# The first token transform on the quarters of the array, with rows loaded by parity

## The chip, the cores and the metric

The kernel runs on one core of one Trainium2 chip. The metric is the device time of one execution in microseconds (us); lower is better. A core has a matrix engine (PE, with its own queue of weight loads, PEld), a vector engine (DVE), a scalar engine (ACT), GpSimd (POOL), a queue that only issues transfers (SP), and 16 DMA engines that all transfers share. SBUF is the memory on the core, 128 partitions wide; PSUM, eight banks of 512 floats in each of 128 partitions, takes the results of PE.

## What is computed

The input x has 2048 tokens of 512 channels (S, D). The reference, cut to what matters:

```python
def _A_ref(x, w_r, w_i):                       # a filter in the spectrum
    X = jnp.fft.rfft2(x, axes=(-2, -1)) * (w_r + 1j * w_i)
    return jnp.fft.irfft2(X, s=(S, D), axes=(-2, -1))

def _B_ref(x, w1, b1, w2, b2):                 # an MLP over the tokens
    h = _layernorm(x)
    u = _gelu(jnp.einsum("bsd,sf->bdf", h, w1) + b1)       # F = 1792
    return (jnp.einsum("bdf,fs->bds", u, w2) + b2).transpose(0, 2, 1)

xn = _layernorm(x)
out = x + _A_ref(xn, w_r, w_i) * _silu(_B_ref(xn, w1, b1, w2, b2))
```

All arrays are 32-bit floats: x and the output 4 MB each, w1 and w2 14.7 MB each, the filter 2.1 MB for each of its two parts.

## The kernel before

**Layout.** Token 16q + j stands at partition q of row block j, so there are 16 row blocks x[:, j] of 128 tokens by 512 channels, and w1[:, j] holds the matching rows of w1. The 1792 columns of w1 are 14 blocks of 128 (NF). The transform over the tokens is split in two steps: a 128-point transform over q within each row block (the first token transform), and 16-point transforms over j later.

**GEMM1** sums, for each of the 14 blocks of w1, over the 16 row blocks. Every operand is split into a high and a low part in a shorter format (ACT makes the high part, DVE the low one), and each product is three matmuls of 128x512: high by high, high by low, low by high. One block takes one PSUM bank, so the blocks go in three groups: the first with the row blocks as they arrive, two more afterwards.

**First stage (lines 429 to 516), a loop over the row blocks j.** For each j: SP loads x[:, j] (load_x, up to five ahead) and two pieces of w1[:, j] (w1_load: WA, four blocks from block 0; WB, three from block 7; three buffers each); DVE and ACT make the mean, the spread and the normalised rows (stats, spreads, scales, normed) and the high and low parts; PE runs 21 matmuls of GEMM1 into banks 0 to 6 (hidden_early) and between them the first token transform into bank 7: four matmuls of 128x128 by 128 columns in full 32-bit floats, where the rows are the weights and a table of cosines and sines, cf (scaled by turned), streams past. ACT copies bank 7 to zt (first_copy), and DVE and POOL add and subtract its quarters into ey (fold). In six of the sixteen passes a further piece of w1 for the second group (w1e, four blocks in two loads of two) is loaded and split ahead of its use. SP also copies x into the output in four pieces, to which results are added at the end.

**Middle (lines 518 to 736).** The last two groups of GEMM1, four blocks (4, 5, 10, 11) and then three (6, 12, 13), run over the same 16 row blocks, in steps of one block and one row block (hidden_rest, hidden). Their w1 pieces, w1s, are loaded up to eight steps ahead (w1_ahead) into four and then five buffers. In between PE runs the filter for eight pairs of frequencies (filter_pair): channel transforms of 128x128, a 16-point transform on 64-row halves (gf), the product with the filter on DVE, and the way back, which is 32 matmuls of 64x64 weights by 64 columns spread over the four quarters of the array (hf by xc). PACE says how many steps of GEMM1 stand between the pieces of the filter. The activation (gelu) and the parts for GEMM2 (forms) follow each block that is complete. The last four row blocks of the last group are kept to the end (LATE, last_sum).

**GEMM2 (line 739 to the end)** runs in 128x256 matmuls with sums of quarters of w2, whose pieces SP and POOL load as buffers come free, with the inverse channel and token transforms (channels, spectral) between.

**What sets the order.** A scheduler orders each engine's instructions; those in keep(...) stand as written. Each engine takes its own in order, SP too: a load that waits for a free buffer holds back all that SP has behind it.

The functions that the diff touches, and what calls them:

Of the kernel before, what the change touches and what calls it, by code (L numbers as in the profile page):

```python
# [3 lines left out]

# [4 lines left out]
F32 = mybir.dt.float32  # L9
# [12 lines left out]
FORMS = (2, 1, 0, 3, 4, 5, 6)  # L22
# [4 lines left out]
PACE = [(2, 2, 2, 1, 1, 1)] * 4 + [(2, 2, 2, 2, 1, 1)] * 4  # L27
# [5 lines left out]
LATE = 12  # L33
# [23 lines left out]
def _constants():  # L57
    q = np.arange(P)
    f = np.zeros((P, P))
    for lo in range(16):  # L60
        for hi in range(4):
            k = _k1(lo, hi)
            a = 2 * np.pi * ((q * k) % P) / P
            f[:, lo * 8 + 2 * hi] = np.cos(a)
            f[:, lo * 8 + 2 * hi + 1] = np.cos(np.pi * q) if k == 0 else np.sin(a)
# [14 lines left out]
    for lo in range(16):  # L80
        for hi in range(4):
            k1, (n, l), (t, h) = _k1(lo, hi), divmod(lo, 2), divmod(hi, 2)
            for r in range(16):
# [14 lines left out]
                rows = slice(64 * t, 64 * t + 64)  # L98
                p = [l * 64 + 2 * (h * 16 + r) + c for c in range(2)]
# [10 lines left out]
    for lo in range(16):  # L110
        for t in range(2):
            rows = slice(64 * (lo % 2), 64 * (lo % 2) + 64)
            v = back[lo // 2, t, rows].reshape(64, 2, 2, 16, 2)
            back[lo // 2, t, rows] = np.einsum("psajb,abhc->pshjc", v, _pairs(lo, t).reshape(2, 2, 2, 2)).reshape(64, 2, 64)

    b = f.T.reshape(32, 2, 2, P)
    even, odd = b[:, 0, :, 0::2].copy(), b[:, 0, :, 1::2].copy()
    even[0], odd[0] = (b[0, 0, 0, 0::2], b[0, 1, 0, 0::2]), (b[0, 0, 0, 1::2], b[0, 1, 1, 1::2])  # L120
    ft = np.concatenate([np.concatenate([v.reshape(64, 64) for v in (even, odd)], 1)] * 2)
# [23 lines left out]
def spectral_mixer_kernel(tc, x, w1, b1, w2, b2, wk, we, wx, c_f, c_ft, c_d, c_i, c_g, c_h, c_t, out):  # L145
# [19 lines left out]
    with tc.tile_pool(name="ps", bufs=1, space=PSUM) as psp, ExitStack() as left, ExitStack() as right:  # L165
        ps = psp.tile([P, 8, 512], F32, name="ps")
        pers = pool(left, "left", "pers", 1)
        cf = pers.tile([P, P], F32, name="cf")
# [75 lines left out]
        def new_h(j):  # L244
            return lnp.tile([P, D], F32, name=f"h{j}", tag="h")

        def turned(j, m, i):

            c = lnp.tile([P, P], F32, name=f"cf{j}", tag="cfj")
            keep(A.activation(c, cf, AF.Copy, scale=m["q"][:, i]))  # L250
            return c

        def first_transform(h, c):
            z = ps[:, 7].rearrange("p (b c) -> p b c", c=P)

            for b, k in enumerate((0, 1, 3, 2)):
                T.matmul(z[:, b], h[:, k * P:(k + 1) * P], c, start=True, stop=True)  # L257
# [16 lines left out]
        def w1_load(j, f0, nf, up, wide):  # L274
            raw = (w1r if up is w1p else up).tile([P, wide * P], F32, name=f"w1r{f0}_{j}", tag="w1r", bufs=3)
            SY.dma_start(raw[:, :nf * P], w1[:, j, f0 * P:(f0 + nf) * P])
# [103 lines left out]
        BATCHES = ((((4, 2), (10, 2)), 4, (7, 2, 0, 1)), (((6, 1), (12, 2)), 3, (7, 0, 1)))  # L380
        w1_early, pairs = {}, {}

        def w1_runs(i, where):
            f = 0
            for f0, nf in BATCHES[i // NJ][0]:
                last = SY.dma_start(where[:, f:f + nf * P], w1[:, i % NJ, f0 * P:(f0 + nf) * P])
# [64 lines left out]
        folds = iter(())  # L451
        for j in range(NJ):
# [18 lines left out]
            z = hidden_early(j, 4, 0, w[0], lambda: first_transform(h, c))  # L471
            hidden_early(j, 3, 4, w[1], lambda: None)
# [43 lines left out]
            folds = fold(j, first_copy(j, z))  # L516
# [531 lines left out]
```

## Time and profile before

| | |
|---|---|
| median of 3 runs | 375.73 us |
| lowest and highest | 375.49 and 379.15 us |
| the profiled execution, as timed | 375.0 us |
| its span in the trace | 373.2 us |
| granted TensorE clock, mean | 0.994 |
| first stage | 7.19 to 98.41 us |
| middle | 98.41 to 207.40 us |
| GEMM2 | 207.40 to 373.2 us |

The profiled execution took 375.0 us, 1.8 us more than the span from its first to its last instruction. It lies 0.7 us under the median. The first stage begins with the first matmul of GEMM1, after 16 matmuls on zeros; the middle with the first matmul on w1e; GEMM2 with the first on parts of w2.

How to read the lines: "x24 | 58.5, 398" is 24 instructions, 58.5 us busy together, 398 ns for one. A line number is that of the kernel; L142 is a helper that records many operations, so there the names of the tiles tell them apart. In the table of stretches each engine has its busy time and its count, and the last three columns are the granted clock, the mean busy share of the 16 DMA engines and the GB/s that they moved. A full-precision matmul shows as two records in the trace.

### The profile page before, as it was taken

Reading aid. Unit: us, or ns where it says so; the run is one execution under the profiler, and the core shown is the slowest. Engines: PE = TensorE matmul, PEld = TensorE weight load, DVE = VectorE, ACT = ScalarE, POOL = GpSimd, SP = SyncE. Lnnn points to the kernel's source line nnn. Section 1 sums busy time; section 2 is a strip of 40 time slices with the busy share of each in tenths; the row PEclk is TensorE's granted clock in tenths of the full one; section 3 lists DMA queues with packets and bytes.
Section 4 is the critical chain, followed back from the end, with each engine's and each line's share of the span. In section 5 each row is a group of like instructions: output and inputs, shape, how many; then the busy total and the mean of one; then the engine's idle time right before and its main releaser. Section 6 shows DMA issues by size and latency. Waiting matters only on the chain.

```text
span 373.2 us, 7614 instructions
## 1 busy us (share of the span) xinstructions
PE 364.3 (98%) x2888; PEld 316.0 (85%) x2888; DVE 296.7 (79%) x565; ACT 212.0 (57%) x381; POOL 84.5 (23%) x123
## 2 busy tenths in 40 slices
PE   8999999999999999999999999999999999999991
PEld 4888888888877777778788999899998989898981
DVE  6799887864298999999999978596868687777871
ACT  4686668654773444456537776545565646564530
POOL 1133322132222221122111001040405050413131
PEclk9999999999999999999999999999999999999997
DMA  7884779304266565787638587897879788887443
GB/s 237 279 293 155 244 240 314 117 0 126 77 191 191 178 226 184 246 259 222 201 84 264 146 232 155 240 134 236 153 212 178 202 188 191 195 190 154 76 56 56
DMA packets 34404, 68.35 MB, mean 183 GB/s; under 512 B 4656, under 2 KB 17856, under 8 KB 34240
## 3 DMA queue, kind: packets, MB, share of 16 engines
q1 hardware_dynamic: 25920, 43.09, 36.1%
q0 software_dynamic: 8448, 24.78, 31.1%
q8 instruction: 22, 0.36, 0.4%
q14 instruction: 14, 0.11, 0.1%
HBM read 59.47 MB, written 8.13 MB: 181 GB/s over the span
## 4 chain that ended last, share of the span: by engine, by line
PE 98%; DVE 0%; POOL 0%; ACT 0%; issue 0%; POOLq 0%
PE ps L142 72%; PE ps L420 21%; PE ps L257 4%; PE ps L409 2%; DVE rows L142 0%; POOL wz L397 0%; ACT g L142 0%; POOLq L1037 0%
## 5 line engine op out<-in xcount | busy, mean ns | idle before, releaser
L142 DVE TENSOR_TENSOR w2f<-a,w2f 128x896 fp32r<-128x896 f32 x36 | 39.3, 1092 | 24.6 <-ACT w2f L142 24.5
L420 PE MATMUL ps<-h,w1h 128*128 128x512 f32 x224 | 58.5, 398 | 0.0
L142 PE MATMUL ps<-h,w1h 128*128 128x512 f32 x176 | 56.2, 401 | 0.0
L420 PEld LDWEIGHTS ps<-h,w1h 128*128 128x128 f32 x224 | 40.9, 188 | 7.9
L142 ACT ACTIVATE w2f<-a 128x896 fp32r<-128x896 f32 x36 | 36.8, 1021 | 12.2 <-issue 6.7
L142 PE MATMUL ps<-fb,w2f 128*128 128x256 f32 x336 | 41.5, 278 | 0.0
L142 PE MATMUL ps<-fa,w2f 128*128 128x256 f32 x336 | 41.0, 277 | 0.0
L142 PEld LDWEIGHTS ps<-h,w1h 128*128 128x128 f32 x176 | 31.6, 188 | 10.7 <-issue 4.9
L142 PEld LDWEIGHTS ps<-fb,w2f 128*128 128x128 f32 x336 | 39.4, 188 | 0.9 <-issue 0.8
L142 PE MATMUL ps<-fc,w2f 128*128 128x256 f32 x336 | 39.6, 276 | 0.0
L142 PEld LDWEIGHTS ps<-fa,w2f 128*128 128x128 f32 x336 | 39.5, 188 | 0.0
L142 POOL DMA_DIRECT2D s<-in_w_dram x14 | 18.2, 1299 | 93.1 <-DMA s<-in_w_dram 60.0
L142 PEld LDWEIGHTS ps<-fc,w2f 128*128 128x128 f32 x336 | 38.9, 188 | 0.0
L142 PE MATMUL ps<-h,w1l 128*128 128x512 f32 x88 | 34.4, 391 | 0.0
L420 PE MATMUL ps<-h,w1l 128*128 128x512 f32 x112 | 30.6, 389 | 0.0
L142 POOL DMA_DIRECT2D out_dram<-r x28 | 23.7, 1285 | 29.8 <-DVE r L142 29.8
L270 POOL TENSOR_TENSOR ey<-t 128x256 f32<-128x256 f32 x16 | 15.7, 982 | 55.1 <-DVE t L268 55.1
L415 DVE TENSOR_TENSOR w1l<-w1r,w1h 128x512 fp32r<-128x512 f32 (+1 forms) x32 | 20.8, 651 | 7.0 <-ACT w1h L412 6.7
L420 PEld LDWEIGHTS ps<-h,w1l 128*128 128x128 f32 x112 | 21.0, 188 | 4.6
L262 ACT ACTIVATE zt<-ps 128x512 f32<-128x512 f32 x16 | 9.5, 595 | 26.2 <-PE ps L257 26.2
L602 POOL DMA_DIRECT2D xc<-xc x16 | 9.8, 620 | 64.0 <-ACT xc L600 47.1
L142 DVE TENSOR_TENSOR w2f<-s,w2f 128x896 fp32r<-128x896 f32 x15 | 16.3, 1088 | 7.9 <-ACT w2f L142 7.9
(115 smaller groups left out, 684.5 us busy)
## 6 DMA issues: line engine op xcount, KB each, us to landing
a<-in_w_dram SPq DMA_DIRECT2D x22, 448.0 KB, 3.8
wt<-in_wk_dram POOLq DMA_DIRECT2D x16, 512.0 KB, 5.1
s<-in_w_dram SPq DMA_DIRECT2D x16, 448.0 KB, 4.0
s<-in_w_dram POOLq DMA_DIRECT2D x16, 448.0 KB, 6.3
w1s<-in_w_dram SPq DMA_DIRECT2D x36, 128.0 KB, 2.8
w1r<-in_w_dram SPq DMA_DIRECT2D x16, 256.0 KB, 4.1
xc<-xc POOLq DMA_DIRECT2D x16, 256.0 KB, 3.0
x<-in_x_dram SPq DMA_DIRECT2D x15, 256.0 KB, 3.3
```

The costliest lines, as they stand in the source:

```text
L142: return lambda *args, **kw: self.keep(operation(*args, **kw))
L257: T.matmul(z[:, b], h[:, k * P:(k + 1) * P], c, start=True, stop=True)
L262: keep(A.activation(zt, z, AF.Copy))
L270: G.tensor_add(ey[:, 0::3, :, j], a, b)
L409: T.matmul(ps[:, 0], wz[:, :P], wz, start=True, stop=True)
L415: keep(V.tensor_sub(dst, src, hi.bitcast(F32)))
L420: T.matmul(ps[:, bank + i], w[wi][:, i * P:(i + 1) * P], hj, start=first and j == 0, stop=last and j == NJ - 1)
L602: keep(G.dma_start(*(v.rearrange("p s t c -> p s (t c)") for v in (there[c::2], here[1 - c::2, ::-1]))))
```

## The change

- **Rows by parity.** Every load of x (first stage) and of w1 goes through by_parity: its source pattern is read as [2, 64, columns], even rows first, so that partitions 0 to 63 hold the even rows of a block and 64 to 127 the odd ones. It is still one load. GEMM1 sums over all rows, so the order does not matter there, as long as x and w1 have the same.
- **First token transform on quarters.** The table cf shrinks from 128x128 to 128x64. A 64-point transform is made of the even rows and of the odd rows apart: sixteen matmuls of 64x64 weights by 64 columns for a row block, two row halves (e, to banks 6 and 7) by two halves of the channels (m) by four blocks of channels. Two row blocks are done behind one another, at every odd j; the last two, 14 and 15, singly. The two halves are put together in the later 16-point tables (gf), where the pairs of frequencies are now formed. ACT's copy of a row block (first_copy) reads both banks and writes runs of two; one copy follows at the end of each pass, so the folds come a pass later for half of the row blocks.
- **GEMM1's blocks six, four, four.** Bank 6 is needed by the transform, so the first stage carries six blocks (0 to 2 and 7 to 9) in place of seven: 18 matmuls a pass. The last two groups have four blocks each (3, 4, 10, 11 and 5, 6, 12, 13), each loaded in two loads of two blocks; the second group had three, of one and two. w1s has four buffers throughout. PACE, LATE, FORMS and the places of gelu are set to the new groups.

The diff, cut to its core:

```diff
-FORMS = (2, 1, 0, 3, 4, 5, 6)
+FORMS = (2, 0, 1, 3, 4, 5, 6)
-PACE = [(2, 2, 2, 1, 1, 1)] * 4 + [(2, 2, 2, 2, 1, 1)] * 4
+PACE = [(2, 2, 2, 2, 2, 1)] * 8
-LATE = 12
+LATE = 4
...
-    f = np.zeros((P, P))
-    for lo in range(16):
-        for hi in range(4):
-            k = _k1(lo, hi)
-            a = 2 * np.pi * ((q * k) % P) / P
-            f[:, lo * 8 + 2 * hi] = np.cos(a)
-            f[:, lo * 8 + 2 * hi + 1] = np.cos(np.pi * q) if k == 0 else np.sin(a)
+    a = 2 * np.pi * (np.outer(q, np.arange(32)) % P) / P
+    f = np.stack([np.cos(a), np.sin(a)], 2)
+    f[0::2, 0, 1], f[1::2, 0, 1] = np.cos(np.pi * q[0::2] / 2), np.sin(np.pi * q[1::2] / 2)
+    f = np.concatenate([f[0::2], f[1::2]]).reshape(P, 64)
...
+                out[:, rows] = np.einsum("sajb,abhc->shjc", out[:, rows].reshape(2, 2, 16, 2),
+                                         _pairs(lo, t).reshape(2, 2, 2, 2)).reshape(2, 64)
...
-        cf = pers.tile([P, P], F32, name="cf")
+        cf = pers.tile([P, 64], F32, name="cf")
...
+        def by_parity(to, src):
+            return SY.dma_start(to, src.rearrange("(q e) c -> e q c", e=2))
         def load_x(j):
             xs[j] = lnp.tile([P, D], F32, name=f"x{j}", tag="x", bufs=5)
-            SY.dma_start(xs[j], x[:, j])
+            by_parity(xs[j], x[:, j])
...
-            return lnp.tile([P, D], F32, name=f"h{j}", tag="h")
+            return lnp.tile([P, D], F32, name=f"h{j}", tag="h", bufs=3)
         def turned(j, m, i):
-            c = lnp.tile([P, P], F32, name=f"cf{j}", tag="cfj")
+            c = lnp.tile([P, 64], F32, name=f"cf{j}", tag="cfj", bufs=3)
             keep(A.activation(c, cf, AF.Copy, scale=m["q"][:, i]))
             return c
-        def first_transform(h, c):
-            z = ps[:, 7].rearrange("p (b c) -> p b c", c=P)
-            for b, k in enumerate((0, 1, 3, 2)):
-                T.matmul(z[:, b], h[:, k * P:(k + 1) * P], c, start=True, stop=True)
-            return z
+        def first_transform():
+            for r, (j, h, c) in reversed(list(enumerate(normal, 2 - len(normal)))):
+                z = ps[:, 6:8, 256 * r:256 * r + 256].rearrange("p e (b c) -> p e b c", b=4)
+                for b, k in enumerate((0, 1, 3, 2)):
+                    for m in range(2):
+                        for e in range(2):
+                            rows, at = slice(64 * e, 64 * e + 64), k * P + 64 * m
+                            T.matmul(z[64 * m:64 * m + 64, e, b], h[rows, at:at + 64], c[rows], start=True, stop=True)
+                transformed.insert(0, (j, z))
+            normal.clear()
         def first_copy(j, z):
             zt = lnp.tile([P, 4, P], F32, name=f"zt{j}", tag="zt")
-            keep(A.activation(zt, z, AF.Copy))
+            keep(A.activation(zt.rearrange("p b (s e c) -> p e (b s) c", e=2, c=2), z.rearrange("p e b (s c) -> p e (b s) c", c=2),
+                              AF.Copy))
             return zt
         def fold(j, zt):
@@ -272,8 +276,8 @@
             yield
         def w1_load(j, f0, nf, up, wide):
-            raw = (w1r if up is w1p else up).tile([P, wide * P], F32, name=f"w1r{f0}_{j}", tag="w1r", bufs=3)
-            SY.dma_start(raw[:, :nf * P], w1[:, j, f0 * P:(f0 + nf) * P])
+            raw = (w1r if up is w1p else up).tile([P, nf * P], F32, name=f"w1r{f0}_{j}", tag="w1r", bufs=3)
+            by_parity(raw[:, :nf * P], w1[:, j, f0 * P:(f0 + nf) * P])
...
-        BATCHES = ((((4, 2), (10, 2)), 4, (7, 2, 0, 1)), (((6, 1), (12, 2)), 3, (7, 0, 1)))
+        BATCHES = (3, (7, 2, 0, 1)), (5, (2, 7, 0, 1))
         w1_early, pairs = {}, {}
-        def w1_runs(i, where):
-            f = 0
-            for f0, nf in BATCHES[i // NJ][0]:
-                last = SY.dma_start(where[:, f:f + nf * P], w1[:, i % NJ, f0 * P:(f0 + nf) * P])
-                f += nf * P
+        def w1_blocks(i, where):
+            f0 = BATCHES[i // NJ][0]
+            for a in range(2):
+                f = (f0 + NH * a) * P
+                last = by_parity(where[:, 2 * P * a:2 * P * (a + 1)], w1[:, i % NJ, f:f + 2 * P])
             return last
         def w1_early_load(i):
             if i % 2 == 0:
                 pairs[i // 2] = usp.tile([P, 2, D], F32, name=f"w1e{i}", tag="u")
-            w1_runs(i, pairs[i // 2][:, i % 2])
+            w1_blocks(i, pairs[i // 2][:, i % 2])
...
-        WA, WB = (0, 4, w1p, 4), (NH, 3, wbp, 3)
+        WA, WB = (0, 3, w1p, 4), (NH, 3, wbp, 3)
         xs[0] = lnp.tile([P, D], F32, name="x0", tag="x", bufs=5)
         halves = slice(0, D // 2), slice(D // 2, D)
         for c_ in halves:
-            SY.dma_start(xs[0][:, c_], x[:, 0, c_])
+            by_parity(xs[0][:, c_], x[:, 0, c_])
...
-        folds = iter(())
+        folds, normal, transformed, copied_rows = iter(()), [], [], []
+        def next_fold():
+            j, z = transformed.pop(0)
+            return fold(j, first_copy(j, z))
...
-            z = hidden_early(j, 4, 0, w[0], lambda: first_transform(h, c))
-            hidden_early(j, 3, 4, w[1], lambda: None)
+            normal.append((j, h, c))
+            hidden_early(j, 3, 0, w[0], first_transform if j % 2 or j == NJ - 2 else lambda: None)
+            hidden_early(j, 3, 3, w[1], lambda: None)
...
-            folds = fold(j, first_copy(j, z))
+            if transformed:
+                copied_rows.append(next_fold())
+                if j == NJ - 3:
+                    copied_rows.append(next_fold())
+                folds = chain(*(copied_rows.pop(0) for _ in range(1 + (j == NJ - 2))))
...
-            n = BATCHES[i // NJ][1] * P
-            if i == NJ:
-                w1_stage.close()
-                w1_raw[0] = pool(lstage, "left", "w1b", 5)
-            loaded[i] = w1_raw[0].tile([P, n], F32, name=f"w1s{i}", tag="w1s")
-            last = w1_runs(i, loaded[i])
+            loaded[i] = w1_raw[0].tile([P, 4 * P], F32, name=f"w1s{i}", tag="w1s")
+            last = w1_blocks(i, loaded[i])
...
-                while ahead and ahead[0] < max(i + AHEAD + (ahead[0] >= NJ), NE + 4):
+                while ahead and ahead[0] < max(i + AHEAD, NE + 4):
                     w1_ahead(ahead.pop(0))
-                j, banks = i % NJ, BATCHES[i // NJ][2]
-                if i == 2 * NJ - LATE // 3:
+                j, banks = i % NJ, BATCHES[i // NJ][1]
+                if i == 2 * NJ - LATE:
...
-        def last_sum(ft, k, bank):
-            for n in range(LATE // 3):
-                hidden(NJ - LATE // 3 + n, k, bank, w1_parts[n])
+        def last_sum(k, bank):
+            for n in range(LATE):
+                hidden(NJ - LATE + n, k, bank, w1_parts[n])
...
-        last_sum(12, 1, 0)
+        last_sum(0, 2)
+        gelu(5, 2)
+        last_sum(2, 0)
...
-        last_sum(13, 2, 1)
+        last_sum(3, 1)
-        last_sum(6, 0, 7)
+        last_sum(1, 7)
```

The first place is SP's queue in the first stage, where the loads of row blocks 2 to 4 stand: x is a row block, w1r a piece of w1 (WA, then WB), in_x_dram and in_w_dram are the arrays in memory, and the last column is the pattern of the destination, partitions first. Before:

```order
L276 DMA w1r_2_281<-in_w_dram 128x512
L276 DMA w1r_2_283<-in_w_dram 128x384
L200 DMA x_331<-in_x_dram 128x512
L276 DMA w1r_3_335<-in_w_dram 128x512
L276 DMA w1r_3_337<-in_w_dram 128x384
L276 DMA w1r_4_410<-in_w_dram 128x512
L465 DMA cd<-in_c_d_dram 128x512
```

The same place now:

```order
L193 DMA w1r_2_272<-in_w_dram 128x1x384
L193 DMA w1r_2_274<-in_w_dram 128x1x384
L193 DMA x_342<-in_x_dram 128x1x512
L193 DMA w1r_3_346<-in_w_dram 128x1x384
L193 DMA w1r_3_348<-in_w_dram 128x1x384
L193 DMA w1r_4_414<-in_w_dram 128x1x384
L474 DMA cd<-in_c_d_dram 128x512
```

The loads stand in the same order and number; the pattern of each load by parity now has three counts, the table cd still two, and the first piece of w1 is a quarter smaller.

The second place is PE in the first stage, row blocks 3 and 4: w1h and w1l are the high and low parts of w1, h those of the rows (or, beside cf, the rows as weights). Before:

```order
L420 MATMUL ps<-h_93,w1h_4_439 128x512 x4
L420 MATMUL ps<-h_93,w1l_4_440 128x512 x4
L257 MATMUL ps<-cf_457,h_443 128x128 x4
L420 MATMUL ps<-h_93,w1h_4_439 128x512 x4
L420 MATMUL ps<-h_93,w1h_4_441 128x512 x3
L420 MATMUL ps<-h_93,w1l_4_442 128x512 x3
L420 MATMUL ps<-h_93,w1h_4_441 128x512 x3
```

Now:

```order
L424 MATMUL ps<-h_92,w1h_3_368 128x512 x3
L424 MATMUL ps<-h_92,w1l_3_369 128x512 x3
L259 MATMUL ps<-cf_398,h_372 64x64 x16
L259 MATMUL ps<-cf_339,h_330 64x64 x16
L424 MATMUL ps<-h_92,w1h_3_368 128x512 x3
L424 MATMUL ps<-h_92,w1h_3_370 128x512 x3
L424 MATMUL ps<-h_92,w1l_3_371 128x512 x3
L424 MATMUL ps<-h_92,w1h_3_370 128x512 x3
L424 MATMUL ps<-h_93,w1h_4_468 128x512 x3
```

A pass has 18 matmuls of GEMM1 in place of 21; every second pass has two transforms of sixteen small matmuls, the others none.

More of the change, by code (lines that the diff above doesn't have):

```diff
@@ L3 @@
 from contextlib import ExitStack
+from itertools import chain
 import concourse.bass as bass
@@ L107, in _constants @@
     freq = freq.reshape(P, 16)
[L110 to L121, printed above, removed]
+    ft = np.concatenate([np.concatenate([f[:64].T, f[64:].T], 1)] * 2)
     c = {
@@ L660, in spectral_mixer_kernel @@
         todo = []
-        late = []
         def form_step():
-            while late:
-                gelu(*late.pop())
             while todo and held[0] + 2 <= passed[0]:
@@ L670, in form_step @@
                 todo.pop(0)
-                late.extend(waiting.pop(0) if waiting else ())
         def hidden_rest():
@@ L695, in hidden_rest @@
                     todo.extend([forms(3), forms(4)])
-                    waiting.append([(5, 2)])
-        def last_sum(ft, k, bank):
-            for n in range(LATE // 3):
-                hidden(NJ - LATE // 3 + n, k, bank, w1_parts[n])
+        def last_sum(k, bank):
+            for n in range(LATE):
+                hidden(NJ - LATE + n, k, bank, w1_parts[n])
         order = [1, 2, 0, 3, 4, 5, 6, 7]
         wts = [weights(2 * order[0])]
-        chain = [filter_pair(n) for n in order]
+        filters = [filter_pair(n) for n in order]
         rest = hidden_rest()
@@ L715, in advance @@
                 else:
-                    next(chain[what[0]])
-        next(chain[0])
-        gelu(9, 6)
+                    next(filters[what[0]])
+        next(filters[0])
+        gelu(9, 5)
         todo.extend(forms(i) for i in FORMS[:3])
-        waiting = [[(3, 3)]]
         advance([START])
-        gelu(8, 5)
-        gelu(7, 4)
+        gelu(7, 3)
+        gelu(8, 4)
         for n in range(8):
```

12 lines of the change are left out of this document (5 added, 7 removed).

## The prediction

> **What bounds the kernel now.** I read the page first: the busy shares, the DMA row of the forty slices, the queues, the chain of work that ended last.
>
> ```profile
> span 373.2 us, 7614 instructions
> PE 364.3 (98%) x2888; PEld 316.0 (85%) x2888; DVE 296.7 (79%) x565; ACT 212.0 (57%) x381; POOL 84.5 (23%) x123
> DMA  7884779304266565787638587897879788887443
> q1 hardware_dynamic: 25920, 43.09, 36.1%
> PE 98%; DVE 0%; POOL 0%; ACT 0%; issue 0%; POOLq 0%
> ```
>
> PE is the bound: it is busy for 98% of the span, and 98% of the chain runs through it. The transfers are hidden, but not by a wide margin: many slices have the DMA engines at 70 to 90%. The queue that SP feeds (q1) moved 43.09 MB and kept sixteen engines busy for 36.1% of 373.2 us, which is 2156 engine-us, so one engine moves 20.0 GB/s. Next the stretches, for the three stages (busy time and count of PE, PEld, DVE, ACT, POOL, then the granted clock, the DMA share and GB/s):
>
> ```profile
> 7.19:98.41 91.22, 91.22 (x467) 77.55 (x465) 69.00 (x187) 59.37 (x125) 23.51 (x34) 1.00 0.58 189
> 98.41:207.40 108.99, 108.99 (x1042) 85.90 (x1041) 101.64 (x179) 61.20 (x113) 22.21 (x39) 1.00 0.65 202
> 207.40:373.20 165.80, 158.18 (x1369) 150.42 (x1367) 122.29 (x187) 88.23 (x140) 37.66 (x44) 0.99 0.74 167
> ```
>
> In the first stage and the middle PE never stops. What the change saves there on PE counts in full, as long as nothing else becomes longer.
>
> **The change on PE.** Two passes of the first stage, and the one place where 32 small matmuls on the quarters stand between full matmuls (start, length, what):
>
> ```profile
> 66.10 1.05 PE L257 MATMUL ps<-cf,h 128*128 128x128 f32 x8
> ...
> 68.62 0.84 PE L420 MATMUL ps<-h,w1l 128*128 128x512 f32 x3
> ...
> 71.79 1.05 PE L257 MATMUL ps<-cf,h 128*128 128x128 f32 x8
> ...
> 185.49 0.39 PE L142 MATMUL ps<-h,w1l 128*128 128x512 f32 x1
> 185.81 1.16 PE L142 MATMUL ps<-hf,xc 64*64 64x64 f32 x64
> 186.90 0.73 PE L142 MATMUL ps<-h,w1h 128*128 128x512 f32 x2
> 187.47 0.40 PE L142 MATMUL ps<-h,w1l 128*128 128x512 f32 x1
> ```
>
> From 68.62 to 71.79 fourteen matmuls of GEMM1 start, 0.2264 us each. A pass lasts 71.79 - 66.10 = 5.69 us; 21 matmuls are 4.75 of it, so a transform costs 0.93. On the quarters, from 185.49 to 187.47, there are three matmuls of GEMM1 (0.68) and 32 small ones of exactly the shape that two row blocks will need: 1.98 - 0.68 = 1.30 us, with the changes of shape in it. Seven pairs save 7 x (2 x 0.93 - 1.30) = 3.9 us. A single transform of sixteen lies between half of 1.30 and all of it, 0.65 to 1.30 against 0.93; I take the middle, no gain, and keep 0.6 us a side for the two together. The number of GEMM1's matmuls is unchanged (14 blocks by 16 by 3); 48 of them, 10.9 us, move from the first stage to the middle. So PE's work falls by 3.9 us, 3.3 to 4.5. ACT's copy and DVE's folds keep their number and size; they move by up to a pass, off PE's path.
>
> **The change on the loads.** This is where I expect the time to be decided. The sizes before (count, KB each, median us to landing):
>
> ```profile
> wt<-in_wk_dram POOLq DMA_DIRECT2D x16, 512.0 KB, 5.1
> w1s<-in_w_dram SPq DMA_DIRECT2D x36, 128.0 KB, 2.8
> w1r<-in_w_dram SPq DMA_DIRECT2D x16, 256.0 KB, 4.1
> xc<-xc POOLq DMA_DIRECT2D x16, 256.0 KB, 3.0
> x<-in_x_dram SPq DMA_DIRECT2D x15, 256.0 KB, 3.3
> out_dram<-in_x_dram SPq DMA_DIRECT2D x4, 960.0 KB, 7.1
> w1r<-in_w_dram SPq DMA_DIRECT2D x16, 192.0 KB, 4.6
> w1e<-in_w_dram SPq DMA_DIRECT2D x12, 128.0 KB, 3.8
> hf<-in_c_h_dram SPq DMA_DIRECT2D x8, 128.0 KB, 2.2
> w1s<-in_w_dram SPq DMA_DIRECT2D x16, 64.0 KB, 3.2
> gf<-in_c_g_dram SPq DMA_DIRECT2D x8, 64.0 KB, 2.0
> x<-in_x_dram SPq DMA_DIRECT2D x2, 128.0 KB
> ```
>
> The x, w1r, w1e and w1s rows add up to 18.87 MB, all of x and w1, and all of it now goes by parity. Before, each such load counts 128 rows first, on both sides. By parity the source counts 2 first, each with 64 rows a step of two apart; the destination still counts 128 partitions. What a load is cut along decides on how many DMA engines it runs. Loads that count 128 first do fill sixteen, as three stretches show (same columns as above):
>
> ```profile
> 20.00:24.00 4.00, 4.00 (x23) 3.46 (x22) 3.72 (x15) 3.39 (x9) 1.62 (x2) 1.00 0.96 295
> 88.00:94.00 6.00, 6.00 (x32) 5.11 (x31) 2.00 (x5) 0.60 (x1) 0.98 (x1) 1.00 0.62 175
> 196.00:200.00 4.00, 4.00 (x78) 3.17 (x77) 3.66 (x10) 1.45 (x3) 0.00 (x0) 1.00 1.01 402
> ```
>
> That the shape of a pattern matters to the hardware is seen at issue: the only loads of before with three counts, four of 2 KB from wx, take longer on SP than loads a hundred times their size (ns, least, median, most):
>
> ```profile
> L586 SPq DMA_DIRECT2D ey<-in_wx_dram x4: 573/603/722, 120.6 to 123.5; - x4
> L276 SPq DMA_DIRECT2D w1r<-in_w_dram x18: 327/382/433, 1.6 to 35.6; - x18
> ```
>
> No row of before shows a large load that counts 2 first. The bounds are two engines (cut along the first count of the source) and sixteen (cut along that of the destination, or along all rows). I take two: both sides must be cut alike, and a first count of 2 can be cut in two at most; the rows show sixteen only where both sides count 128 first. The Trainium skill, page "DMA: Bandwidth & Descriptors", section "Why a DMA increments its semaphore by 16 and not by 1", has it as a rule: a transfer runs on the largest number of engines, up to 16, that divides the slowest dimension of both patterns. Here that gives two, and a sum of 722; with sixteen engines the sum is 371. The trace agrees for 128 (a share of 1.01); no run here shows it for 2.
>
> With two engines the sum is one of transfers, since PE, ACT and DVE then wait for x and w1. Line by line:
>
> - Start of the first load: 1 us.
> - 18.87 MB at two engines of 20.0 GB/s: 472 us. The three stretches bound an engine: 175 / (16 x 0.62) = 17.6 GB/s, with runs of 1 KB (w1s), and 402 / (16 x 1.01) = 24.9, with runs of 3.5 KB from w2. By parity the runs are 1 KB (w1e, w1s), 1.5 KB (w1r) and 2 KB (x), between these, and 20.0 is the mean of the queue. That is 536 to 379 us.
> - Everything else takes a sixteenth of its bytes from each of those two engines while they are full: out, wt, xc, hf and gf, 1.13 MB in all a sixteenth, and small tables, 57 us (46 to 65).
> - SP takes its queue in order, and behind hf and gf, which wait for PE, stand w1s loads:
>
> ```profile
> SPq L594 <- PE ps L142: 15.8, 6, 8.9
> SPq L571 <- PE ps L142: 8.7, 4, 7.3
> 183.33 10.35 SPq L386 DMA_DIRECT2D w1s<-in_w_dram  x8
> ```
>
>   Those waits are 24.5 us before; loads that are already queued hide part of them. I take half, 12 us (0 to 24.5). SP's issue itself, at 0.6 us for some 100 loads in place of 0.38, is 22 us more on a queue that waits for buffers anyway: nothing.
> - From the last w1s load to GEMM2: the last issue ends at 193.7, the load lands 2.8 us later, GEMM2 starts at 207.4: 10.9 us. The kept row blocks are four as before, now with four blocks each: 3 us more at most, of which the first matmuls can run before the last load. I take 11 + 1.
> - GEMM2, whose loads are unchanged: 165.8 us.
> - Around the span: 1.8 us.
>
> Sum: 1 + 472 + 57 + 12 + 12 + 165.8 + 1.8 = 721.6 us against the profiled execution's 375.0; the median lies 0.7 higher, so 722. The ends: 1 + 379 + 46 + 0 + 11 + 165.8 + 1.8 = 605, and 1 + 536 + 65 + 24.5 + 14 + 165.8 + 1.8 = 808. PE's 3.9 us are inside its waits and count for nothing. The same page, section "Specifications", gives about 27 GiB/s for an engine; by that estimate the parity loads take 325 us and the sum is some 560. The best stretch above gives 24.9.
>
> **The rivals.**
>
> - *The loads still run on sixteen engines, and PE stays the bound.* Then the sum is PE's: 375.0 - 3.9 = 371.1, 371.8 against the median, faster by 1.0%. For it: one load is issued, as before, and the destination still counts 128. Against it: the first count of the source. It decides from the point where the loads keep up: the first stage needs x, w1r and w1e, 12.06 MB, in 7.2 + 16 x 18 x 0.2264 + 7 x 1.30 + 2 x 0.9 = 83 us, which is 145 GB/s or 7.3 engines. From eight engines on this rival holds; below seven the loads decide.
> - *Sixteen engines, but DVE becomes the bound in the six passes with w1e.* Two such passes:
>
> ```profile
> 43.36:54.73 11.37, 11.37 (x60) 9.67 (x58) 9.51 (x26) 8.01 (x17) 3.21 (x4) 1.00 0.76 262
> L415 DVE TENSOR_TENSOR w1l<-w1r,w1h 128x512 fp32r<-128x512 f32 x16 | 12.0, 751 | 7.0 <-ACT w1h L412 6.7 <-ACT cf L250 0.3
> L415 DVE TENSOR_TENSOR w1l<-w1r,w1h 128x384 fp32r<-128x384 f32 x16 | 8.8, 551 | 0.0
> ```
>
>   DVE has 9.51 us of work there, less 2 x 0.20 for the smaller w1l: 9.1. PE's two passes shrink to 36 x 0.2264 + 1.30 = 9.45. If DVE keeps its idle 1.86 us as well, a pair lasts 11.0 and loses 1.5, three pairs 4.6: 375.7. For it: DVE is at 96%. Against it: DVE ran ahead by several us in the passes before, and its idle time was waiting for PE.
> - *Two engines, but faster ones.* A pair that alone uses the memory might do better than the queue's mean; the low end, 605, is priced with the best stretch. This is in the main case.
>
> **How the numbers follow.** Two engines: 0.86, with 722 as the time and 605 to 808 as bounds, which hold 0.93 of it, so 0.80 of all. Sixteen engines with PE as the bound: 0.06 (371 to 372). Sixteen with DVE late: 0.06 (372 to 376). Some number between: 0.02 (376 to 600). The range is therefore 605 to 808 and leaves out both rivals. A measurement of this kernel can tell about 1% from no change. Faster by over 1%: two thirds of the first rival, 0.04. Within 1%: the rest of it and the second, 0.08. Slower: 0.88.
>
> **What would show it.** In the changed kernel's forty slices the DMA row should stand at 1 or 2 for some three quarters of the span, with 35 to 50 GB/s, and at its old height only in GEMM2; the busy share of PE falls to about half. x should take over 8 us to land in place of 3.3 (256 KB at 40 GB/s is 6.6 us, on top of a start of about 2, the time that gf takes). The idle time of ACT, DVE and PE should be put down to DMA on x, w1r and w1s. A pair of transforms should take about 1.3 us, or less where PE waits around it. If instead the DMA row reads 5 to 9 from the start and x lands in 3 to 4 us, the main case is wrong and the first stage's end tells the rivals apart: near 83 us for the first, near 88 for the second. If the share is low but the GB/s are above 50, only the rate of an engine was mis-sized.

## The result, and the profile after

The changed kernel takes 653.56 us (median of 4 runs, 652.95 to 657.9) against 376.04 us of the kernel before (4 runs, 375.49 to 379.15): 1.7375 times as long, 95% interval 1.7254 to 1.7497. The profiled execution took 652.95 us.

GEMM2, which the change doesn't touch, lasts about 166 us in some executions of the kernels here and about 170 in others, so that the kernel before itself comes out at 375 or at 379 us, and where a few us matter I compare the time at which GEMM2 starts.

The page of the changed kernel, for the lines shown of before (the chain last):

```profile
span 651.2 us, 8387 instructions
...
PE 426.8 (66%) x3272; PEld 341.2 (52%) x3272; DVE 301.5 (46%) x565; ACT 212.4 (33%) x381; POOL 80.7 (12%) x123
...
PEclk7776685677677568876989968998589999999999
DMA  1111112111121221023543432333357778888744
GB/s 39 48 50 49 66 46 101 48 48 48 47 103 47 102 74 75 31 74 100 181 144 124 143 99 99 131 110 100 107 124 182 194 168 192 179 200 207 175 78 64
...
q1 hardware_dynamic: 24338, 43.05, 20.0%
...
DMA 42%; PE 31%; SPq 17%; DVE 6%; ACT 2%; issue 1%; ACTq 0%; DVEq 0%
```

The span is 278 us longer, the bytes of q1 are nearly the same (43.05 MB, 43.09 before), and PE's share of the chain fell from 98% to 31%. In the first 16 slices (260 us) the DMA row stands at 1 or 2, and nine of those slices read 46 to 50 GB/s, which fits two engines at work; the first experiment below counts them. The old height returns only in GEMM2. The stages (same columns as in the prediction):

```profile
0.00:273.15 273.15, 123.26 (x816) 84.77 (x817) 72.74 (x199) 61.79 (x130) 19.56 (x38) 0.71 0.17 60
273.15:484.70 211.55, 144.71 (x1089) 105.36 (x1088) 106.39 (x181) 62.55 (x113) 23.48 (x41) 0.83 0.36 115
484.70:651.20 166.50, 158.81 (x1369) 151.07 (x1367) 122.39 (x186) 88.04 (x140) 37.70 (x44) 0.99 0.74 166
```

All the time was lost ahead of GEMM2: it starts at 484.70 in place of 207.40 us, and then lasts 166.5 against 165.8. What the engines waited for (us in total, times, longest):

```profile
ACT w1h L416 <- DMA w1r<-in_w_dram: 179.0, 32, 14.2
ACT w1h L151 <- DMA w1s<-in_w_dram: 116.7, 20, 9.6
PE ps L424 <- ACT w1h L416: 116.5, 18, 18.8
DVE stm L210 <- DMA x<-in_x_dram: 35.9, 6, 10.0
```

The first row is the transfer of w1 that ACT waits for, the third PE waiting for ACT in turn. These are the loads that went by parity.

### The profile page after: what moved, and what is told of

The parts are those of the page before. It is cut to its first block, busy times and chain, and to the rows that moved or that the text cites. A ratio compares the mean times of both kernels' runs of the same rounds, so it can differ in the third digit from the quotient of the medians.

```text
span 651.2 us, 8387 instructions
## 1 busy us (share of the span) xinstructions
PE 426.8 (66%) x3272; PEld 341.2 (52%) x3272; DVE 301.5 (46%) x565; ACT 212.4 (33%) x381; POOL 80.7 (12%) x123
## 3 DMA queue, kind: packets, MB, share of 16 engines
q1 hardware_dynamic: 24338, 43.05, 20.0%
## 4 chain that ended last, share of the span: by engine, by line
DMA 42%; PE 31%; SPq 17%; DVE 6%; ACT 2%; issue 1%; ACTq 0%; DVEq 0%
PE ps L135 30%; DMA w1r<-in_w_dram 25%; SPq L193 14%; DMA w1s<-in_w_dram 12%; DMA gf<-in_c_g_dram 3%; DMA x<-in_x_dram 2%; SPq L468 1%; SPq L410 1%; DVE xc L628 1%; DVE xc L627 1%; SPq L595 1%; DVE xc L625 1%; ACT w1h L151 1%; DVE xc L630 1%; DVE stm L210 1%
## 5 line engine op out<-in xcount | busy, mean ns | idle before, releaser
L424 PE MATMUL ps<-h,w1h 128*128 128x512 f32 x192 | 76.0, 525 | 116.5 <-ACT w1h L416 116.5
L424 PEld LDWEIGHTS ps<-h,w1h 128*128 128x128 f32 x192 | 45.7, 254 | 137.7 <-ACT w1h L416 128.0
L419 DVE TENSOR_TENSOR w1l<-w1r,w1h 128x384 fp32r<-128x384 f32 x32 | 17.9, 558 | 160.3 <-ACT w1h L416 160.3
L135 PE MATMUL ps<-h,w1h 128*128 128x512 f32 x208 | 75.0, 445 | 16.5 <-ACT w1h L151 16.5
L416 ACT ACTIVATE w1h<-w1r 128x384 fp32r<-128x384 f32 x32 | 16.7, 522 | 179.0 <-DMA w1r<-in_w_dram 179.0
L135 PEld LDWEIGHTS ps<-h,w1h 128*128 128x128 f32 x208 | 42.2, 214 | 35.3 <-ACT w1h L151 19.4
L151 ACT ACTIVATE w1h<-w1s 128x512 fp32r<-128x512 f32 x26 | 16.4, 629 | 121.8 <-DMA w1s<-in_w_dram 116.7
L151 DVE TENSOR_TENSOR w1l<-w1s,w1h 128x512 fp32r<-128x512 f32 x26 | 17.8, 688 | 72.4 <-ACT w1h L151 72.3
L135 DVE TENSOR_TENSOR w2f<-a,w2f 128x896 fp32r<-128x896 f32 x36 | 39.3, 1092 | 24.9 <-ACT w2f L135 24.8
L135 PE MATMUL ps<-h,w1l 128*128 128x512 f32 x104 | 44.1, 424 | 1.6 <-DVE w1l L151 1.6
L424 PE MATMUL ps<-h,w1l 128*128 128x512 f32 x96 | 38.8, 525 | 8.1 <-DVE w1l L419 8.1
L135 PE MATMUL ps<-sh,gf 64*64 64x512 f32 x64 | 16.7, 851 | 39.0 <-ACT sh L588 34.4
L274 POOL TENSOR_TENSOR ey<-t 128x256 f32<-128x256 f32 x16 | 15.6, 973 | 207.0 <-DVE t L272 207.0
L424 PEld LDWEIGHTS ps<-h,w1l 128*128 128x128 f32 x96 | 25.2, 267 | 16.3 <-DVE w1l L419 9.7
```

The costliest lines, as they stand in the source:

```text
L135: return lambda *args, **kw: self.keep(operation(*args, **kw))
L151: return A.activation(hi, src, AF.Copy), V.tensor_sub(lo, src, hi.bitcast(F32))
L274: G.tensor_add(ey[:, 0::3, :, j], a, b)
L416: keep(A.activation(dst, src, AF.Copy))
L419: keep(V.tensor_sub(dst, src, hi.bitcast(F32)))
L424: T.matmul(ps[:, bank + i], w[wi][:, i * P:(i + 1) * P], hj, start=first and j == 0, stop=last and j == NJ - 1)
```

## The experiments

**Does the shape of the load alone cost the time?** The kernel before, with nothing changed but the order of the rows in its loads of x and w1; the transform, its table's columns and GEMM1's groups stay. REST = 2 is the order of the change; 4, 8 and 16 sort the rows by a larger rest, so that the source counts 4, 8 or 16 first. It is still one load each time, with the same bytes and the same runs.

```diff
+        def by_rest(to, src):
+            return SY.dma_start(to, src.rearrange("(q e) c -> e q c", e=REST))
...
-            SY.dma_start(xs[j], x[:, j])
+            by_rest(xs[j], x[:, j])
...
-        "c_f": f.astype(np.float32),
+        "c_f": f[np.arange(P).reshape(-1, REST).T.ravel()].astype(np.float32),
```

Two:

> The kernel before, with nothing changed but the order of rows in the loads of x and w1: even rows first, then odd, in one load (source pattern [2, 64, columns]); the table cf has its rows in the same order. Theory: two engines, 18.87 MB at about 49 GB/s, so 640 to 670 us, with the whole loss and none of the rest of the change. Rival (the loss comes from the transform or the new order): 376 us.

Four:

> As e2_rest2, but rows by their remainder by 4 (source pattern [4, 32, columns]). Theory, first count of the source gives the engines: four engines, about 98 GB/s. The first stage needs 13.1 MB of x, w1r and w1e, 134 us and some 10 for other transfers in place of 91; the middle needs 5.8 MB, 59 us, and has 109: hidden. So 375 + 54 = about 430 us (415 to 450). Rival (three counts in a pattern are slow as such, whatever the first): as slow as e2_rest2, 640 to 670. Rival (only parity itself, row steps of two, is slow in memory): 376.

Eight:

> As e2_rest2, but rows by their remainder by 8 (source pattern [8, 16, columns]). Theory: eight engines, about 196 GB/s; 13.1 MB take 67 us, under the 91 of the first stage. The prediction put the point from which the loads keep up at 7.3 engines, so 376 to 385 us, with the start a few us later. Rival (three counts are slow as such): 640 us or more.

Sixteen:

> As e2_rest2, but rows by their remainder by 16 (source pattern [16, 8, columns]). Theory: sixteen engines, so the time of the kernel before within 1%, and what is left of the difference is the longer issue of a pattern with three counts (0.6 us in place of 0.38). Rival (the engines go by something else than the first count): slower than e4_rest8.

Measured: 650.5 us with two (one run), 455.4 with four (one run), 382.8 with eight (4 runs, ratio 1.014, 1.0069 to 1.0211), 380.1 with sixteen (one run, beside 376.0 of before; GEMM2 lasts 170 us in it). The same 40 us of the first stage, from the kernel before and then from REST = 2, 4, 8 and 16 (the last columns are the clock, the mean share of the DMA engines and GB/s):

```profile
20.00:60.00 40.00, 40.00 (x206) 34.01 (x205) 35.54 (x95) 28.90 (x62) 12.80 (x16) 1.00 0.72 238
```

```profile
20.00:60.00 40.00, 17.76 (x54) 13.01 (x54) 9.41 (x30) 6.49 (x14) 1.74 (x5) 0.67 0.14 49
```

```profile
20.00:60.00 40.00, 29.19 (x125) 22.93 (x124) 20.44 (x59) 15.08 (x32) 5.04 (x10) 0.88 0.34 120
```

```profile
20.00:60.00 40.00, 40.00 (x205) 33.97 (x204) 35.32 (x94) 29.87 (x64) 12.48 (x16) 1.00 0.62 220
```

```profile
20.00:60.00 40.00, 40.00 (x206) 34.01 (x205) 35.92 (x96) 29.57 (x64) 12.82 (x16) 1.00 0.91 250
```

The row order alone makes the loss: 650.5 us without any other part of the change, 653.6 with all of it. The rate grows with the first count of the source, 49, 120, 220, 250 GB/s, the share of the engines with it, and PE's busy time in the stretch is back at 40 of 40 us from eight on. The engines can be counted as well. By the traces' records of single transfers, in these 40 us never fewer than two are under way with REST = 2, four with 4 and eight with 8; just two are under way for 35.6 us, just four for 26.3 and just eight for 19.7. With sixteen it is sixteen or more for 28.1 us. In the changed kernel it is just two for 33.1 us.

Four came out 5 us above what I had expected; the runs don't show why. Eight is just short of enough: its GEMM2 starts at 212.56 us against 207.40, that of sixteen at 207.95. The Trainium skill, page "DMA: Bandwidth & Descriptors", section "Why a DMA increments its semaphore by 16 and not by 1", has the largest number up to 16 that divides the slowest dimension on both sides; the four sizes agree with it.

**Two loads in place of one.** In the changed kernel each parity load becomes two loads of 64 rows, so that each counts 64 first on both sides.

```diff
         def by_parity(to, src):
-            return SY.dma_start(to, src.rearrange("(q e) c -> e q c", e=2))
+            for e in range(2):
+                last = SY.dma_start(to[64 * e:64 * e + 64], src[e::2])
+            return last
```

> The changed kernel, but each load by parity is issued as two loads, of the 64 even and of the 64 odd rows; every other instruction is the same. Theory (the one load, cut along its first count of 2, ran on two DMA engines and everything waited for it): both loads count 64 first and run on sixteen engines, the DMA row of the slices is back at 5 to 9 in the first stage, and the time is that of PE's sum, 371 to 373 us. Rival (the loss comes from the small matmuls on the quarters, from both banks of the transform being in use at once, or from the new order of GEMM1): 600 us or more, as the changed kernel. A third possibility: SP now issues some ten loads in a pass with w1e, about 4.5 us of a pass of 4.7, and falls behind: 376 to 390 us.

Measured: 396.75 us (6 runs), ratio 1.0512 (1.0441 to 1.0583). Of the loss of 278 us some 20 are left, more than the third possibility allowed, and a new limit stands in its place. The issue of w1r's loads on SP (ns, least, median, most; first and last start), before and here:

```profile
L276 SPq DMA_DIRECT2D w1r<-in_w_dram x32: 327/380/433, 1.6 to 71.8; - x32
```

```profile
L194 SPq DMA_DIRECT2D w1r<-in_w_dram x64: 465/594/1652, 3.3 to 90.5; - x64
```

A load took SP 380 ns before and takes 594 here, and there are twice as many. SP issued almost without a break until 91 us; the first stage ended at 105.48 us (88.37 in the joined kernel below, which has the same matmuls).

To see whether it is the issue, the odd rows' loads were given to POOL:

```diff
-                last = SY.dma_start(to[64 * e:64 * e + 64], src[e::2])
+                last = (SY, G)[e].dma_start(to[64 * e:64 * e + 64], src[e::2])
```

> As e1_two_loads, with the same loads of 64 rows, but those of the odd rows are issued by POOL in place of SP. Theory (SP's issue is the bound in e1_two_loads): SP has 5 loads in a pass with w1e, 3.1 us, POOL 5 and its own 1.5 us of work, some 4.5 us of a pass of 4.7; the first stage falls from 97.5 to 77 to 85 us and the ratio to 0.985 to 1.015. Rival (the loads of 64 rows themselves are slow): no change against e1_two_loads, 1.05.

Measured: 378.68 us (10 runs), ratio 1.0046 (0.9997 to 1.0094); the first stage takes 81.8 us, as the theory had it. And the counterpart: the kernel before, rows in their old order, each load cut in two loads of 64 neighbouring rows:

```diff
+            for e in range(2):
+                SY.dma_start(to[64 * e:64 * e + 64], src[64 * e:64 * e + 64])
```

> The kernel before, with its order of rows, but each load of x and w1 issued as two loads of 64 neighbouring rows: SP's doubled issue alone, without parity, quarters or a new grouping. Theory: 122 loads of 0.6 us and some 10 us of others are 85 us of SP for a first stage of 91, but in the passes with w1e ten loads are 6.2 us for a pass of 5.7; a small loss at the start and there: ratio 1.00 to 1.02. Rival (loads of 64 rows slow as such): above 1.04.

Measured: 394.88 us (4 runs), ratio 1.0444 (1.0378 to 1.0509), which is more than I had expected:

```profile
L200 SPq DMA_DIRECT2D w1r<-in_w_dram x64: 465/594/1237, 3.3 to 90.8; - x64
```

The kernel before, whose PE never stopped, loses 4.4% by the doubled loads alone, at the same 594 ns, with its issues spread to 90.8 us in place of 71.8. By the number alone the rival, that loads of 64 rows are slow as such, had come true; but the kernel with two queues has the same loads of 64 rows and loses next to nothing. So of the 5.1% of the two loads nearly all is their number on one queue. The Trainium skill, page "DMA: Bandwidth & Descriptors", section "Issuing engines are not separate DMA queues", says that issuing on several engines only saves the time of initiating, usually small beside the transfer. It did save just that here (1.0512 to 1.0046), but the time was not small: one queue's issue was what bound the stage.

**As few loads as before.** Two loads by rows, but both pieces of w1 that a pass needs are joined in one load of [64, 2, columns]:

```diff
+        def both_halves(to, i, f0, nf):
+            return by_parity(to, w1[:, i].rearrange("p (a c) -> p a c", a=2)[:, :, f0 * P:(f0 + nf) * P])
...
-                raws[j + 1, 0], raws[j + 1, 1] = w1_load(j + 1, *WA), w1_load(j + 1, *WB)
+                raws[j + 1, 0], raws[j + 1, 1] = w1_load(j + 1)
```

> As e1_two_loads, but the pieces of w1 that are loaded at the same time (WA and WB; the two pieces of a w1e or w1s) go in one load for the even and one for the odd rows (source pattern [64, 2, columns]). SP issues 6 loads in a pass with w1e where e1_two_loads issues 10. In e1_two_loads SP issued without a break up to 91 us, 0.6 us a load, and the first stage took 97.5 us where PE's sum has 76. Theory (there SP's issue was the bound, and the DMA engines and the quarters were not): 6 loads are 3.7 us of a pass of 4.7, SP keeps ahead, the first stage takes 76 to 79 us, and the kernel is faster than before: 0.985 to 0.995 of it, 371 to 374 us where before has 376. Rival (loads of 64 rows are slow on the DMA engines, or DVE is the bound in the passes with w1e): the first stage stays above 85 us and the ratio above 1.01.

Measured: 378.77 us (12 runs), ratio 1.0033 (0.9986 to 1.0079). Neither side was met (the first stage takes 80.3 us): the loads no longer hold PE back for long, but the gain on PE isn't there. PE's rows that follow a wait (start, length, what, and in brackets the wait):

```profile
8.09 0.96 PE L425 MATMUL ps<-h,w1h 128*128 128x512 f32 x3 [1.64 <-ACT w1h L417]
9.81 0.96 PE L425 MATMUL ps<-h,w1l 128*128 128x512 f32 x3 [0.76 <-DVE w1l L420]
20.22 0.96 PE L425 MATMUL ps<-h,w1h 128*128 128x512 f32 x3 [0.70 <-ACT w1h L417]
25.90 0.98 PE L425 MATMUL ps<-h,w1l 128*128 128x512 f32 x3 [0.36 <-DVE w1l L420]
...
208.28 2.63 PE L135 MATMUL ps<-fd,w2f 128*128 128x256 f32 x21
```

PE starts 0.9 us later than before (7.19) and waits in the first four passes (the brackets understate it, since the ends of matmuls are modelled). From the first matmul to GEMM2 there are 200.19 us, before 200.21: what the quarters save has gone into waits. I first took SP's issues at the start for the cause, and gave half of them, in the first three passes, to POOL:

```diff
+                queue = G if e and len(raws) <= 4 else SY
-                last = SY.dma_start(to[64 * e:64 * e + 64], src[e::2])
+                last = queue.dma_start(to[64 * e:64 * e + 64], src[e::2])
```

> The joined loads, with the odd rows' halves of the first three passes' loads of x and w1 issued by POOL and all others by SP. Theory: the transform on the quarters does save its 3.8 us, and the joined kernel lost them at the beginning, where PE starts 0.9 us later and then waits about 4 us more for x and w1r that SP issues at 0.6 us each. With half of these issues on POOL the start goes back to about 7.4 us and most of the 4 us go: GEMM2 starts 2 to 4 us earlier than at 208.3, and the ratio is 0.990 to 0.998. Rival: the waits are for something else (DVE's work ahead of the first matmuls, or the transfers themselves), and GEMM2 starts at 207.5 or later with a ratio of 1.000 or more.

Measured: 378.02 us (12 runs), ratio 1.0043 (1.0007 to 1.0078), GEMM2 at 208.76 us. My theory fell: PE did start earlier, and the waits only moved. PE, then the instructions of ACT ahead of the waits:

```profile
7.68 0.93 PE L426 MATMUL ps<-h,w1h 128*128 128x512 f32 x3 [1.24 <-DVE h L242]
...
14.43 0.97 PE L426 MATMUL ps<-h,w1h 128*128 128x512 f32 x3 [1.50 <-ACT w1h L418]
...
20.84 0.97 PE L426 MATMUL ps<-h,w1h 128*128 128x512 f32 x3 [0.67 <-ACT w1h L418]
```

```profile
11.97 0.35 ACT L250 ACTIVATE cf<-cf,qm 128x64 f32<-128x64 f32 x1 [2.08 <-POOL qm L234]
12.22 1.08 ACT L238 ACTIVATE h<-x,nbm,rsm 128x256 f32<-128x256 f32 x2
13.33 0.63 ACT L418 ACTIVATE h<-h 128x512 fp32r<-128x512 f32 x1
13.87 0.92 ACT L418 ACTIVATE w1h<-w1r 128x384 fp32r<-128x384 f32 x2
...
17.29 0.20 ACT L219 ACTIVATE sdm<-v2m 128x4 f32<-128x4 f32 x1 [2.26 <-DVE v2m L218]
18.62 1.09 ACT L238 ACTIVATE h<-x,nbm,rsm 128x256 f32<-128x256 f32 x2 [1.13 <-DVE nbm L231]
...
20.29 0.92 ACT L418 ACTIVATE w1h<-w1r 128x384 fp32r<-128x384 f32 x2
```

The high part of w1 comes late because ACT waits for POOL's and DVE's small operations of the row statistics, not for a transfer. So the next theory: the passes without a transform are now 18 matmuls, 4.1 us, against 5.7 before, and in the first ones PE overtakes the chain that makes a row block ready. To test it, row blocks 1 to 3 are normalized with row block 0's mean and scale; their own statistics are left out, so the result isn't the reference's:

```diff
-        m1 = moments("m1", 1)
-        stats(m1, 0, xs[1])
...
-        spreads(m1, 1)
...
-        scales(m1)
...
-        of = {1: (m1, 0)}
...
+        of = {1: (m, 0), 2: (m, 0), 3: (m, 0)}
...
```

> The joined kernel with POOL's help at the beginning; row blocks 1 to 3 are normalized with row block 0's mean and scale, so that DVE's, ACT's and POOL's statistics of these three blocks are left out (the output is therefore not the reference's); nothing else is changed. Theory: with passes of 4.1 us in place of 5.7 PE catches up with the chain of small operations that makes the first row blocks (statistics, square root, scale, normalized rows, high and low parts), and this costs about what the quarters save. Without the statistics of blocks 1 to 3 PE's idle time after its first matmul falls from some 3 us to under 1.5, GEMM2 starts at 203.5 to 206.5 in place of 208.8, and the ratio is 0.987 to 0.998. Rival: PE waits for transfers of x and w1r. Then GEMM2 still starts at 208 or later, with a ratio of 1.002 or more.

> The kernel before with the same statistics left out, as the counterpart: PE does not wait there after its first matmul, so by both theories nothing changes. Theory and rival: GEMM2 starts at 207.0 to 207.8, ratio 0.998 to 1.002. If it became faster by 1% the statistics would bound the kernel before as well, and the comparison with the joined kernel would say nothing.

Measured: the joined kernel 375.64 us (10 runs), ratio 0.9954 (0.9905 to 1.0003); the kernel before with the same left out 376.21 us (10 runs), ratio 1.0 (0.9954 to 1.0047). The joined one:

```profile
7.80 0.93 PE L426 MATMUL ps<-h,w1h 128*128 128x512 f32 x3 [0.46 <-DVE h L242]
...
13.47 1.16 PE L262 MATMUL ps<-cf,h 64*64 64x64 f32 x64
...
22.95 1.16 PE L262 MATMUL ps<-cf,h 64*64 64x64 f32 x64
...
205.05 2.64 PE L135 MATMUL ps<-fd,w2f 128*128 128x256 f32 x21
```

and the kernel before:

```profile
7.01 1.27 PE L420 MATMUL ps<-h,w1h 128*128 128x512 f32 x4
...
207.18 2.64 PE L142 MATMUL ps<-fd,w2f 128*128 128x256 f32 x21
```

The waits after the start are gone but for 0.2 us, and GEMM2 starts at 205.05, 3.7 us earlier than with the statistics, as the theory had it, while before is unmoved (207.18). From the first matmul to GEMM2 it is 197.25 against 200.17 us, so 2.9 of the forecast 3.9 us come through; where the last one went isn't shown. By these traces, one execution of each kernel, the statistics of the first blocks are what the gain was lost to; the ratio of the times agrees but its interval just touches 1. No version that computes everything was faster than the kernel before.

## Why the prediction was right, and which terms were off

The forecast was 722 us in a range of 605 to 808; 653.56 lies in it, by the mechanism that was named. One term was mis-sized, the rate of an engine, and it accounts for nearly all of the 68 us between forecast and median.

- **Two engines: right.** The load's shape alone gives 650.5 us, the rate follows its first count, and two transfers are under way at a time. The decision point of 7.3 engines was worked out with 20.0 GB/s an engine; with the 24.5 below it is 5.9. The runs say only that four are too few and that eight still cost 1.4%.
- **"18.87 MB at two engines of 20.0 GB/s: 472 us": mis-sized.** The nine slices show 46 to 50 GB/s, some 24.5 for an engine, near the best stretch (24.9), which the prediction had kept as the low end. Up to 473.5 us, when the last w1s load has landed, 39.7 MB were moved, 18.87 of them by parity; with a sixteenth of the other 20.9 each of the two engines moved 10.74 MB. Fewer than two transfers were under way for only 10.9 us of that time (from 1 us on), so the two engines worked for 461.6 us, at 23.3 GB/s. The prediction had 472 + 57 = 529. Part of the gap is the measure: by bytes over busy share, as the prediction took it, the row of REST = 2 has 49 / (16 x 0.14) = 21.9, since the share counts somewhat more than two engines. Why it was 20.0 with all sixteen at work, the runs don't show. The Trainium skill, page "DMA: Bandwidth & Descriptors", section "Specifications", gives about 27 GiB/s for an engine, from which the prediction's estimate of 560 was worked out; that lies above what was measured.
- **The others' sixteenth: 57 us** comes out at 56 of these 461.6: 1.30 MB in place of 1.13 and the small tables, at the faster rate.
- **"SP's issue itself … nothing": right, but not for its reason, a queue that waits for buffers.** SP was held for as long as the two engines take to drain a load (ns, least, median, most):

```profile
L193 SPq DMA_DIRECT2D w1s<-in_w_dram x52: 513/2841/6488, 274.3 to 461.2; - x52
L193 SPq DMA_DIRECT2D w1r<-in_w_dram x32: 522/3672/6717, 2.1 to 252.2; - x32
L193 SPq DMA_DIRECT2D x<-in_x_dram x17: 519/3009/7355, 0.7 to 219.8; - x17
```

  Before it was 380 ns for w1r. At 49 GB/s the 128 KB of a w1s load are 2.7 us, and SP needed 2.8. The two engines had work all the while, so as far as the records show this hold adds nothing to their time. A small load that stands behind does come late. From the middle, on SP and then on PE:

```profile
308.28 4.16 SPq L193 DMA_DIRECT2D w1s<-in_w_dram  x1
312.54 3.94 SPq L580 DMA_DIRECT2D gf<-in_c_g_dram  x1
...
326.88 1.83 PE L135 MATMUL ps<-sh,gf 64*64 64x512 f32 x8 [4.56 <-DMA gf<-in_c_g_dram]
```

  The table gf has 64 KB, and its issue took 0.33 us before; here it took 3.9, and PE waited 4.6 us for the table to land. But PE is not the bound there. Its wait of 15.6 us at the beginning of the middle is one for w1s itself: ACT, which takes its work in order, has the filter's sh behind a high part of w1 that waits for its load; the table had landed, since two of the eight records of the matmuls that read it stand at 280.5.

```profile
295.98 0.63 ACT L151 ACTIVATE w1h<-w1s 128x512 fp32r<-128x512 f32 x1 [5.24 <-DMA w1s<-in_w_dram]
296.52 0.58 ACT L588 ACTIVATE sh<-ps 128x512 f32<-128x512 f32 x1
...
297.15 1.98 PE L135 MATMUL ps<-sh,gf 64*64 64x512 f32 x6 [15.58 <-ACT sh L588]
```

- **SP's waits: 12 us** became the 10.9 in which fewer than two transfers were under way. The size is right by luck: the prediction looked for them behind hf and gf, and 7.2 of them lie at the end of the first stage, where SP waits first for DVE's last low part and then for PE's last matmuls before it goes on to the loads of the middle (us in total, times, longest):

```profile
SPq L566 <- DVE w1l L419: 13.2, 1, 13.2
SPq L566 <- PE ps L424: 3.8, 1, 3.8
```

- **From the last w1s load to GEMM2: 12 us** became 11.2, counted from the landing at 473.5 to 484.7.
- **GEMM2 and around the span:** 165.8 became 166.5; 1.8 stayed. With these the sum is 1 + 461.6 + 10.9 + 11.2 + 166.5 + 1.8 = 653.0. The terms split the measured span, so the sum is no test; the size of each beside its forecast is.
- **The transform on PE: right.** In the changed kernel it can't be read, with the clock low. In the joined kernel without the statistics two passes last 22.95 - 13.47 = 9.48 us; 36 matmuls of 0.2264 are 8.15 of it, so a pair costs 1.33 us, forecast 1.30, against 1.86 for two before. It was worth nothing here, first behind the loads, then, with these mended, behind the row statistics.
- **The rivals.** Both began with sixteen engines, and the changed kernel had two. With the loads mended, the first, 371.8 us with PE as the bound, was not reached by any kernel's median. The second named the right kind of mechanism for the joined kernel, the engines ahead of PE being late; but it looked for it in the passes with w1e, and it came in the first four.
- **The signs.** The waits of ACT, DVE and PE were put down to w1r, w1s and x, as forecast; how long x took to land the page doesn't give. PE was to be busy "about half"; it shows 66%, since the granted clock fell (below) and the same matmuls lasted longer. The DMA row stands at 1 or 2 for 16 slices of 40 and at 2 to 5 in the middle, not "three quarters of the span": the middle had the two engines at work too, but beside them POOL's queue moved 14.4 of the middle's 24.3 MB, in bursts with sixteen and more transfers under way, so that the row shows more.

## What to carry to other kernels

Before the row order or the shape of a load is changed, look at what its pattern counts first (here only the source's count was varied): with the same loads in bytes and runs the transfers went from 238 to 49 GB/s when the source counted 2 first, and eight were just short of what feeds this kernel. The repair by more loads has a price on the queue that issues them; joining pieces, or a second queue, took nearly all of it away here. And a saving on the engine that bounds the kernel counts only where the engines that feed it are ahead: here they were, except in the first four passes, and these took all of it.

## What the runs showed of the hardware

- SP's issue of a load grew as fewer engines drained it: a w1r load that SP issues in 0.38 us before took a median of 3.7 with two engines (most 6.7) and 1.8 with four (w1r in the REST = 4 kernel); with eight it was 0.60, hardly more than the 0.55 with sixteen.
- The issue itself depends on the shape. The medians for x and w1r are 0.34 and 0.38 us for 128 rows, 0.53 (with POOL issuing half) to 0.59 for 64 rows, and 0.54 to 0.61 for 128 rows with three counts (REST = 16 and 8). With sixteen engines the longer issue hid; with twice the loads on one queue it did not.
- The granted clock of PE fell where PE waited: 0.71 as the mean of the first stage (1.00 before). The same GEMM1 matmul then lasted 525 ns as against 398:

```profile
L424 PE MATMUL ps<-h,w1h 128*128 128x512 f32 x192 | 76.0, 525 | 116.5 <-ACT w1h L416 116.5
```

  It can have cost little, since PE waited for loads anyway, but a busy share read from such a trace overstates the work.
